# One core, attention with global tokens and a softplus layer: other operands for the fillers, an earlier hold for the loads of batch 1, and a new order of 1,721 jobs

## The chip, the cores and the metric

The kernel runs on one core of a Trainium2 chip. The metric is the device time in microseconds (us) of one execution, the median of several runs. The engines named below are PE (matrix multiply), PEld (its weight loads), DVE (vector), ACT (scalar, with table functions), POOL (general purpose) and SP (which issues most of the loads). A letter q behind an engine's name means its queue of instructions, where DMAs are issued.

## The reference

Eight batches of eight heads of attention, 576 tokens, 64 wide. A token sees its neighbours within 32 positions and eight global tokens; global tokens see everything. Then a two-layer network with softplus over all 4608 tokens.

```python
# q, k, v: (8, 8, 576, 64) float32; global_idx: 8 positions
scores = scale * np.matmul(q, k.transpose(0, 1, 3, 2))
mask = np.abs(pos[:, None] - pos[None, :]) <= 32
mask = mask | is_global[:, None] | is_global[None, :]
scores = np.where(mask, scores, -1000000000.0)
scores = scores - np.max(scores, axis=-1, keepdims=True)
attn = np.exp(scores)
attn = attn / (np.sum(attn, axis=-1, keepdims=True) + 1e-09)
out = np.matmul(attn, v)
# x: (4608, 512), the heads side by side; w_in (512, 2048), w_out (2048, 512)
h = x @ w_in
g = np.maximum(h, 0.0) + np.log1p(np.exp(-np.abs(h)))
return (g @ w_out).astype(np.float32)
```

## The kernel before

**Units of work.** A batch is 18 blocks of 32 tokens. A "pair" is four blocks (128 tokens); there are 36 pairs, and four pairs make one of nine stages m of 512 tokens. For each pair: scores `sc` into PSUM (with the mask added by a matmul `mk` in the first four pairs, by DVE `ma` in the others), row maximum `mx`, subtraction `sub` (not in the first four), exponential `ex`, sum and reciprocal `su`, normalisation `no`, transpose `tp`. The first four pairs do `mx` to `no` in two halves of four heads each. For each batch: loads of q, k and v into `stage` (tiles used by one batch after another), rounding `cast` into `qb`, `kb`, `vb`, transposes into `qx` and `kx`, picking out the global keys and queries (`pick`, `put`, `fill`, `gev`), and the global tokens' own attention: scores `sg`, maximum `mxg`, exponential `gexp`, transpose `tpg` into `pgt`, product `ov`, then `odd`, `both`, `gv`. For the stage: `val` multiplies the probabilities with v into PSUM tiles `xo`, `xev` copies them into xT, the first layer is 16 chunks `h` of four matmuls each, `soft` the softplus into `g`, the second layer `o` four tiles of 16 matmuls, `oev` copies to `osb`, and a DMA stores.

**Batches 0 and 1** are special: q and k come in three pieces each (token ranges t = 0, 1 of 256 tokens, t = 2 of 64), their transposes `tr` are done by PE with an identity, and `trev` (named `turn` in the lists below) copies them out. Stage 0 goes through `val`, `xev` and `h` in three parts of 128, 256 and 128 tokens (`val_0`, `val_1`, `val_2`), stage 1 in two.

**The order.** Each of these steps is a job with a rough cost on each engine that can do it. `_Order` has a list ORDER with one number for each job: five times the job's number plus the engine (0 PE, 1 ACT, 2 DVE, 3 POOL, 4 loads issued by SP). The program walks this list, keeps a clock for each engine from the costs, and emits the jobs in the order of the clock's times. So on each engine the order is that of the list; the modelled times only decide which of the eight PSUM banks a tile takes and where PE fillers stand. Each engine then runs its jobs strictly in order and waits with semaphores for the others.

**Fillers.** Where the model has PE idle for 0.7 us or more, before 34 us of modelled time, `keep` puts in matmuls `warm` that nobody reads: 55% of the gap divided by 220 ns each. Their operands are the first 512 columns of `pgt`, cleared at the start; `pgt` is also where batch 0's `tpg` writes.

**Loads and holds.** SP issues q, k and v; POOL issues the four pieces of `w_in` and the four of `w_out` (each a weight piece converted to 16 bits on the way). Where a load is meant to stay behind a weight piece, `follow` issues a tiny DMA that reads the last values of that piece, so that SP stands still until it has landed. For batch 1 `follow(0, w_in_t[1])` is called with piece x == 0 of the list FIRST, which is q's t = 0; and `follow(1, w_out_t[1])` with half h == 0 of v. The v halves are also made to depend on job `w_out` 1 in the list. The tiny `landed` copy on POOL waits for k's t = 1 of batch 1, and the `w_out` pieces stand behind it.

The order of SP's loads before: batch 0: k t0, k t1, k t2, q t0, q t2, q t1, v half 0, v half 1; batch 1: k t0, k t2, q t0, k t1, q t1, q t2, v half 1, v half 0; then k and q of batch 2, and so on.

Of the kernel before, what the change touches and what calls it, by code (L numbers as in the profile page):

```python
# [19 lines left out]
class _Order:  # L20
# [82 lines left out]
    SHARE = 0.12  # L103
# [27 lines left out]
    WARM = 0  # L131
# [155 lines left out]
def kernel(  # L287
# [242 lines left out]
    if WARM:  # L530
        clear(nc.vector, pgt[:].rearrange("p m i h -> p (m i h)")[:, 0:512])
# [145 lines left out]
    def act(n, psum=True):  # L677
        t = (137 if psum else 270) + .9 * n
        return t - 98, t
# [25 lines left out]
    def fill_in(key, n, thin):  # L705
        ps = psum(key, [P, 512], FP32)
        w = P if thin else 4 * P
        for x in range(n):
            nc.tensor.matmul(out=ps[:, 0:w], lhsT=idle[:, 0:P], rhs=idle[:, 0:w], start=True, stop=True)  # L709
# [39 lines left out]
    def add_parts(b):  # L749
        last = None  # L750
        for x, (w, t) in enumerate(FIRST[b]):
            def emit(e, x=x, w=w, t=t):
                if x == 0 and b:
                    follow(0, w_in_t[1])
# [675 lines left out]
```

## Time and profile before

| | us |
|---|---|
| median of 3 runs (lowest, highest) | 337.99 (337.87, 338.98) |
| the profiled execution | 338.2 |
| its span in the trace | 336.5 |
| PE busy | 316.2 |
| DVE, ACT, POOL busy | 250.0, 224.2, 179.1 |
| mean granted PE clock | 0.975 |

The span runs from the first to the last instruction of the trace; the rest of the execution's time lies around it. Rows of instructions in order of time give the start, the length, the engine, the source line, the operation, output and inputs, and in brackets how long the engine was idle ahead of it and who released it. Lines that stand for several steps: L700 is every copy between tiles, told apart by the tile's name; L1246 is `h`, L1257 `o`, L1211 `val`, L709 the fillers, L1044 the scores, L969 `ov`, L824 the key and query transposes, L958 `tpg`, L1099 `no`, L1108 `tp`, L1080 `ex` of the first four pairs (eight short instructions, of which four carry one half's values and four read the sums), L953 `gexp`, L1067 `sub`, L732 the tiny DMA of `follow`, L494 and L498 the pieces of batches 0 and 1, L444 and L449 the other q, k and v loads, L1308 and L1312 the weights.

### The profile page before, as it was taken

What the parts mean: (1) busy time and instruction counts of PE and PEld (TensorE: products, weight loads), DVE (VectorE), ACT (ScalarE), POOL (GpSimd) and SP (SyncE); (2) the same over time, 40 slices, a digit from 0 to 9 for tenths busy, and PEclk for the clock granted to TensorE, in tenths of its full rate; (3) what the DMA queues carried; (4) which work ended last, traced back from release to release, by engine and by line L of the source; (5) the groups of instructions that cost most, each with busy time, mean ns of one, the idle gap of its engine ahead of it and who ended that gap; (6) DMA issues with size and microseconds to landing.
All of it is one profiled execution on the core that took longest, in us unless ns stands there. A gap on an engine that the chain in (4) does not pass through costs nothing.

```text
span 336.5 us, 12158 instructions
## 1 busy us (share of the span) xinstructions
PE 316.2 (94%) x5286; PEld 170.0 (51%) x5333; DVE 250.0 (74%) x416; ACT 224.2 (67%) x456; POOL 179.1 (53%) x159
## 2 busy tenths in 40 slices
PE   7669899889999999999999999999999999999996
PEld 3426786466555444554554445444544454454453
DVE  6688589968899899998986688788779878460000
ACT  3787767786786859287836786698467665945541
POOL 5554708986386479729865747496631823200000
PEclk9756999999999999999999999999999999999999
DMA  7999998999955989992988997401310030010002
GB/s 182 229 217 238 202 172 138 155 182 193 168 91 103 171 185 174 163 190 59 185 140 167 231 177 176 104 33 49 91 65 2 33 128 33 0 64 33 31 16 109
DMA packets 168733, 42.74 MB, mean 127 GB/s; under 512 B 153192, under 2 KB 165736, under 8 KB 168680
## 3 DMA queue, kind: packets, MB, share of 16 engines
q1 hardware_dynamic: 160664, 28.33, 47.5%
q0 software_dynamic: 6144, 10.49, 13.0%
q10 hardware_dynamic: 1872, 3.15, 2.5%
q8 instruction: 41, 0.67, 0.8%
q14 instruction: 12, 0.10, 0.1%
HBM read 36.71 MB, written 9.44 MB: 137 GB/s over the span
## 4 chain that ended last, share of the span: by engine, by line
PE 61%; DVE 9%; SPq 8%; DMA 8%; POOL 6%; issue 5%; ACT 1%; DVEq 0%; POOLq 0%
PE h L1246 26%; PE o L1257 24%; SPq L444 6%; PE xo L1211 3%; PE s L1044 3%; DMA wout<-in_moe_w_out_dram 3%; POOL pn L1099 2%; DMA stage<-in_q_dram 2%; DMA stage<-in_k_dram 2%; DVE st L1048 2%; DVE m L1061 1%; PE ov L969 1%; DMA stage<-in_v_dram 1%; POOL qb L697 1%; PE warm L709 1%
## 5 line engine op out<-in xcount | busy, mean ns | idle before, releaser
L1246 PE MATMUL h<-xT,win 128*128 128x512 bf16 (+3 forms) x758 | 132.5, 325 | 1.9 <-issue 0.5
L1257 PE MATMUL o<-wout,g 128*128 128x512 bf16 (+1 forms) x560 | 128.3, 373 | 4.7 <-issue 3.3
L1252 ACT ACTIVATE g<-h 128x512 bf16<-128x512 f32 (+3 forms) x192 | 84.3, 500 | 42.2 <-PE h L1246 40.7
L1246 PEld LDWEIGHTS <-win 128*128 128x128 bf16 x768 | 66.5, 98 | 59.4 <-issue 1.4
L1257 PEld LDWEIGHTS <-g 128*128 128x128 bf16 x592 | 55.5, 98 | 62.3 <-issue 1.6
L1067 POOL TENSOR_TENSOR st<-st,m 128x1024 f32<-128x1024 f32 x27 | 52.1, 1933 | 58.0 <-DVE m L1061 49.0
L1099 POOL TENSOR_TENSOR pn<-st,rs 128x1024 bf16<-128x1024 f32 (+1 forms) x32 | 56.7, 1776 | 33.0 <-DVE rs L1093 27.3
L1048 DVE TENSOR_TENSOR st<-s,mask 128x512 f32<-128x512 f32 x64 | 41.1, 676 | 6.9 <-PE s L1044 6.7
L1091 DVE TENSOR_REDUCE sm<-st 128x8 f32<-128x1024 f32 x32 | 38.4, 1199 | 7.3 <-ACT st L1084 7.2
L1061 DVE TENSOR_REDUCE m<-st 128x8 f32<-128x1024 f32 x32 | 38.1, 1201 | 0.3
L1084 ACT ACTIVATE st<-st 128x1024 f32<-128x1024 f32 x32 | 32.7, 1057 | 2.9 <-POOL st L1067 2.3
L700 ACT COPY osb<-o 128x512 f32<-128x512 f32 (+1 forms) x27 | 15.3, 571 | 20.1 <-PE o L1257 15.1
L1108 DVE STREAM_TRANSPOSE pt<-pn 128x512 int32<-128x512 int32 x36 | 24.4, 690 | 3.6 <-POOL pn L1099 3.4
L700 DVE CAST xT<-xo 128x512 bf16<-128x512 f32 (+3 forms) x23 | 12.1, 564 | 13.6 <-PE xo L1211 13.4
L700 ACT CAST xT<-xo 128x512 bf16<-128x512 f32 (+3 forms) x25 | 10.6, 474 | 16.3 <-PE xo L1211 16.1
L697 POOL TENSOR_SCALAR qb<-stage 128x1152 bf16<-128x1152 f32 (+1 forms) x11 | 14.5, 1315 | 9.3 <-DMA stage<-in_q_dram 6.6
L700 POOL CAST kb<-stage 128x1152 bf16<-128x1152 f32 (+1 forms) x12 | 17.2, 1455 | 3.0 <-DMA stage<-in_k_dram 3.0
L1044 PE MATMUL s<-kx,qx 64*32 64x128 bf16 x1152 | 15.8, 229 | 2.1 <-DVE qx L700 0.8
L1044 PEld LDWEIGHTS <-qx 64*32 64x32 bf16 x1152 | 10.9, 94 | 13.3 <-issue 8.9
L1269 POOL DMA_DIRECT2D out_dram<-osb x24 | 14.5, 603 | 5.0 <-ACT osb L700 5.0
L953 ACT ACTIVATE pg<-sg,gnb 128x320 bf16<-128x320 f32 (+1 forms) x32 | 14.9, 581 | 1.5 <-DVE gnb L947 1.5
L1252 ACT ACT_TABLE_LOAD x12 | 15.4, 1283 | 0.7 <-PE h L1246 0.5
(125 smaller groups left out, 312.0 us busy)
## 6 DMA issues: line engine op xcount, KB each, us to landing
stage<-in_v_dram SPq DMA_DIRECT2D x64, 144.0 KB, 4.5
stage<-in_k_dram SPq DMA_DIRECT2D x48, 144.0 KB, 4.3
stage<-in_q_dram SPq DMA_DIRECT2D x48, 144.0 KB, 3.8
out_dram<-osb POOLq DMA_DIRECT2D x24, 256.0 KB, 3.3
out_dram<-osb ACTq DMA_DIRECT2D x11, 256.0 KB, 2.3
stage<-in_k_dram SPq DMA_DIRECT2D x4, 512.0 KB, 6.1
stage<-in_q_dram SPq DMA_DIRECT2D x4, 512.0 KB, 5.6
win<-in_moe_w_in_dram POOLq DMA_DIRECT2D x4, 512.0 KB, 11.2
```

What stands on the lines that cost most here:

```text
L700: {"ACT": nc.scalar.copy, "DVE": V.tensor_copy, "POOL": nc.gpsimd.tensor_copy}[e](out, in_)
L1044: nc.tensor.matmul(out=PS["s", n, g][quad(a ^ g), x, :], lhsT=qx[b % 2][rows(g), a, j * BL:(j + 1) * BL], rhs=kx[b % 2][rows(g), a, e0 * B ...
L1048: V.tensor_tensor(out=PS["st", n][:, h, :, :], in0=PS["s", n, h][:, :, :], in1=mask[:, h, j0:j0 + PB, :, :].rearrange("p j s i -> p j (s i ...
L1061: V.reduce_max(out=m[:], in_=flat(PS["st", n], h0, h1), axis=AX)
L1067: on(e).tensor_tensor(out=t, in0=t, in1=over(PS["m", n, y][:], SL * BL), op=OP.subtract)
L1084: nc.scalar.activation(out=t, in_=t, func=AF.Exp)
L1091: V.reduce_sum(out=sm[:], in_=flat(PS["st", n], h0, h1), axis=AX)
L1099: on(e).tensor_tensor(out=PS["pn", n][:, :, :, h0:h1].rearrange("p x s h -> p h x s"), in0=PS["st", n][:, h0:h1], in1=PS["rs", n, y][:].re ...
L1108: V.transpose(out=bass.AP(base.tensor, base.offset, ap=[list(base.ap[0]), [2 * STEP, PB // 2], [STEP + BL // 2, 2], [1, SL * BL]]), in_=PS ...
L1246: nc.tensor.matmul(out=h[:, :], lhsT=w_in_t[c // 4][:, kd, c % 4 * P:(c % 4 + 1) * P], rhs=PS["xT", m][:, kd, lo:hi], start=(kd == 0), sto ...
L1252: nc.scalar.activation(out=PS["g", m, c][:, lo:hi], in_=PS[key][:, lo_of(c, hi - lo)], func=AF.Softplus)
L1257: nc.tensor.matmul(out=PS["o", m, ns, a][:, :], lhsT=PS["g", m, kf][:, ns * P:(ns + 1) * P], rhs=w_out_t[kf // 4][:, kf % 4, a:z], start=( ...
```

## The change

The fillers read `vb[1]` (four blocks of 128 columns, cleared by DVE at the start) and no longer `pgt`. `follow` now acts once for each of its two tiles, at whichever load comes first in the list: for batch 1 that is the first piece of q or k, behind `w_in` 1, and the first half of v, behind `w_out` 0 instead of 1. Modelled costs of many jobs are other numbers, and so is the share that SP's loads get when both queues run (SHARE). ORDER is a new list throughout; the jobs are the same 1,721, of which 103 are on another engine (as an example, `no` from DVE to POOL five times and back four times, `sub` from POOL to DVE six times and back three times, `xev` 13 times from DVE to ACT and 11 times back). In counts: PE 891 jobs as before, ACT 351 (346), DVE 309 (311), POOL 130 (133), loads 40 as before.

```diff
-    SHARE = 0.12
+    SHARE = 0.55
...
     if WARM:
-        clear(nc.vector, pgt[:].rearrange("p m i h -> p (m i h)")[:, 0:512])
+        nc.vector.memset(vb[1][:, 0:4, 0:2 * D], 0.0)
...
-    idle = pgt[:].rearrange("p m i h -> p (m i h)")
+    idle = vb[1][:, 0:4, 0:2 * D]
...
-            nc.tensor.matmul(out=ps[:, 0:w], lhsT=idle[:, 0:P], rhs=idle[:, 0:w], start=True, stop=True)
+            nc.tensor.matmul(out=ps[:, 0:w], lhsT=idle[:, 0, :], rhs=idle[:, 0, :] if thin else idle, start=True, stop=True)
...
+    followed = set()
+
     def follow(x, t):
+        if x in followed:
+            return
+        followed.add(x)
         nc.sync.dma_start(out=trail[x:x + 1, :], in_=t[0:1, t.shape[1] - 1, t.shape[2] - 2:])

     def add_load(b, w, deps):
-        behind = had(("w_out", 1)) if b == 1 else []
+        behind = had(("w_out", 0)) if b == 1 else []
...
-                    if behind and h == 0:
-                        follow(1, w_out_t[1])
+                    if behind:
+                        follow(1, w_out_t[0])
...
-                if x == 0 and b:
+                if b:
                     follow(0, w_in_t[1])
...
-                T["half", b, h] = o.add({"DMA": (2200 if b else 0, 0)}, emit, deps, rank=0, moves=4000 if b else 2700 + 600 * h, late=LATE if b else 0)
+                T["half", b, h] = o.add({"DMA": (2200 if b else 0, 0)}, emit, deps, rank=0, moves=3300 if b else 2500 + 1100 * h, late=LATE if b else 0)
...
-            T["ex", n, y] = o.add({"ACT": act(k, False) if not masked else (1050, 1150) if n in SUMMED else (1390, 1490)}, lambda e, y=y: ex(e, y), [job, *gate],
+            T["ex", n, y] = o.add({"ACT": act(k, False) if not masked else (1050, 1150) if n in SUMMED else (1390, 1420)}, lambda e, y=y: ex(e, y), [job, *gate],
...
-    for job in o.run(dict(PE=1200 if WARM else 3000, ACT=2600, DVE=2100, POOL=3400, DMA=2700)):
+    for job in o.run(dict(PE=1200 if WARM else 3000, ACT=2600, DVE=2100, POOL=3400, DMA=2300)):
```

What the two lists say for the start, decoded (names as above; the digits behind `ex`, `mx`, `su`, `no` are pair and half, `tr b w t` is batch, 0 for q or 1 for k, token range; "h[128:384]" is a chunk of the second part):

| engine | before | after |
|---|---|---|
| PE | k transposes of batch 0; q t0; mk 0, sc 0; q t2, q t1; mk 1, sc 1; sg 0; sc 3, sc 2; ov 0; val_0; 16 chunks h; val_1; tr 1 k t0; six chunks h[128:384]; val_2; tr 1 q t0; tr 1 k t1, t2; ... sc 5, sc 4 | k transposes of batch 0; mk 0, mk 1; q t0, q t2; sc 0, sc 1; q t1; sg 0; sc 2, sc 3; ov 0; val_0; 11 chunks h; tr 1 k t0; 1 chunk; val_1; tr 1 k t1; 4 chunks; six chunks h[128:384]; val_2; tr 1 q t0; tr 1 k t2; q t2; three chunks; sc 4, sc 5 |
| ACT | ex 0 and ex 1 (both halves); gexp 0; ex 3 (both); ex 2,0; gv 0; two xev 0; ex 2,1; soft | ex 0 and ex 1 (both halves); gexp 0; ex 2,1; odd 0; ex 2,0; ex 3 (both); two xev 0; soft |
| DVE | mxg 0; ...; su 1,1; mx 3,1; tpg 0; mx 3,0; su 0,1; mx 2,1; mx 2,0; odd 0; both 0; tp 0; su 1,0; no 1,0; ... no 3 (both); tp 3; tp 2; casts of batch 1 | mxg 0; mx 2,1; su 1 (both); mx 2,0; tpg 0; su 0,1; mx 3 (both); both 0; gv 0; tp 0; ... tp 1; su 3,0; no 3 (both); tp 2; two casts of k t0; tp 3; a cast of k t1; one xev 1; the cast of k t2; one xev 1 |
| POOL | w_in 0, 1, 2; one cast of v; no 0,0; w_in 3; no 0,1; no 1,1; no 2 (both); clears of batch 1's tiles; three casts of batch 1; landed; w_out 0, 1; a cast; w_out 2; sub 5; sub 4; w_out 3 | w_in 0, 1; two casts of v; w_in 2; no 0 (both); no 1,0; w_in 3; no 1,1; no 2 (both); clears of batch 1's tiles; landed; a cast of k t1; w_out 0, 1, 2; four casts of q; w_out 3; sub 5; sub 4 |
| SP, batch 1 | k t0, k t2, q t0, k t1, q t1, q t2, v 1, v 0 | k t0, k t1, k t2, q t0, q t2, q t1, v 1, v 0 |

In both lists the end is the same: the last tiles of `o`, their copies on ACT and the stores.

More of the change, by code (lines that the diff above doesn't have):

```diff
@@ L746, in add_load @@
             T["load", b, w] = o.add({"DMA": (4400, 0)}, lambda e: load_qk(nc.sync, b, w, (0, 2, 1, 3)), deps, rank=0,
-                                    moves=9200 if w else 8800, late=LATE, behind=had(("load", b - 1, 2)) if b == EARLY else [])
+                                    moves=8500 if b == EARLY else 9000, late=LATE, behind=had(("load", b - 1, 2)) if b == EARLY else [])
     def add_parts(b):
@@ L896, in add_prep @@
                     T["cast", b, w].append(job)
-                    T["turn", b, w][t].append(o.add({"DVE": dve(n), "ACT": act(n)}, lambda eng, w=w, t=t, e=e: trev(eng, w, t, e),
+                    T["turn", b, w][t].append(o.add({"DVE": (620, 710) if t < FULL else (200, 280), "ACT": (630, 740) if t < FULL else (280, 380)}, lambda eng, w=w, t=t, e=e: trev(eng, w, t, e),
                                                     [T["last", w]], rank=at, uses=[k_]))
@@ L911, in add_prep @@
         T["fill", b] = o.add({"DVE": (430, 510), "ACT": (430, 520)}, fill, [T["put", b, 1]] + blanked, rank=rank - 1 if b else 0, uses=[kkey], lead=0 if b else LEAD)
-        T["gev", b] = o.add({"DVE": (150, 240), "ACT": (230, 340)}, gev, [T["put", b]] + blanked, rank=rank - 1 if b else 0, uses=[qkey], lead=0 if b else LEAD)
+        T["gev", b] = o.add({"DVE": (110, 195), "ACT": (150, 200)}, gev, [T["put", b]] + blanked, rank=rank - 1 if b else 0, uses=[qkey], lead=0 if b else LEAD)
     def turned(b, j0, j1):
@@ L990, in add_global @@
         lead = 0 if b else LEAD
-        T["sg", b] = o.add({"PE": (380, 550)}, sg, [x for y in T["turn", b, 1] for x in (y if b < EARLY else [y])] + had(("fill", b), ("gev", b)) + gate, rank=3, array=64, ins=32,
+        T["sg", b] = o.add({"PE": (380, 440) if b else (570, 700)}, sg, [x for y in T["turn", b, 1] for x in (y if b < EARLY else [y])] + had(("fill", b), ("gev", b)) + gate, rank=3, array=64, ins=32,
                            opens=[("sg", key) for key in keys], lead=lead)
@@ L1114, in add_pair @@
         if apart:
-            T["mk", n] = o.add({"PE": (660, 830)}, mk, T["mask"], rank=2, ins=4, opens=[("s", ("s", n, h)) for h in range(2)])
-            T["sc", n] = o.add({"PE": (450, 620)}, sc, ready + had(("mk", n)), rank=0, array=64, ins=64,
+            T["mk", n] = o.add({"PE": (910, 1010)}, mk, T["mask"], rank=2, ins=4, opens=[("s", ("s", n, h)) for h in range(2)])
+            T["sc", n] = o.add({"PE": (550, 630)}, sc, ready + had(("mk", n)), rank=0, array=64, ins=64,
                                uses=[("s", n, h) for h in range(2)], opens=[("st", ("st", n))])
         else:
-            T["sc", n] = o.add({"PE": (280 + 540 * masked, 450 + 540 * masked)}, sc, ready + (T["mask"] + had("make_ends")[:n // TP] if masked else []), rank=3, array=64, ins=64 + 4 * masked,
+            T["sc", n] = o.add({"PE": (280 + 700 * masked, 450 + 700 * masked)}, sc, ready + (T["mask"] + had("make_ends")[:n // TP] if masked else []), rank=3, array=64, ins=64 + 4 * masked,
                                opens=[("s", ("s", n, h)) for h in range(2)] + [("st", ("st", n))])
@@ L1321 @@
     setup("make_band", lambda e: make_band(), {"DVE": (1000, 1080)}, rank=0)
-    setup("make_ident", lambda e: make_ident(), {"DVE": (200, 280)}, [T["make_band"]], rank=0)
+    setup("make_ident", lambda e: make_ident(), {"DVE": (250, 400)}, [T["make_band"]], rank=0)
     setup("make_hot", lambda e: make_hot(), {"DVE": (500, 580)}, [T["make_ident"]], rank=0)
@@ L1329 @@
     setup("make_neg", lambda e: make_neg(), pool(1250), [], rank=0)
-    setup("make_edges", lambda e: make_edges(), {"DVE": (330, 400)}, [T["make_ident"]], rank=1)
+    setup("make_edges", lambda e: make_edges(), {"DVE": (110, 190)}, [T["make_ident"]], rank=1)
     T["slots"] = []
@@ L1391 @@
                 T["w_out", a] = o.add({"POOL": (800, 0)}, lambda e, a=a: weights_out(a),
-                                      [T["landed"], T.get(("w_out", a - 1))], rank=-1, hold=800 if a else 0, moves=3200)
+                                      [T["landed"], T.get(("w_out", a - 1))], rank=-1, hold=800 if a else 0, moves=3100)
         for x in range(len(VALS)):
```

20 lines of the change are left out of this document (10 added, 10 removed), and 144 rows, old and new, of the table ORDER.

## The prediction

> **What bounds the kernel now.** First the shares of the page, then the busy time by stretch (columns: stretch, its length, busy time and instruction count of PE, PEld, DVE, ACT, POOL, the granted PE clock, the DMA share, GB/s).
>
> ```profile
> PE 316.2 (94%) x5286; PEld 170.0 (51%) x5333; DVE 250.0 (74%) x416; ACT 224.2 (67%) x456; POOL 179.1 (53%) x159
> ...
> 10.00:20.00 10.00, 6.31 (x148) 4.01 (x150) 7.53 (x18) 7.81 (x33) 6.63 (x11) 0.67 1.30 227
> 20.00:30.00 10.00, 7.47 (x150) 2.93 (x152) 8.54 (x22) 7.78 (x38) 3.84 (x5) 0.50 1.24 203
> 30.00:40.00 10.00, 8.90 (x236) 7.93 (x239) 7.13 (x17) 7.69 (x31) 8.00 (x15) 0.98 1.13 238
> ...
> 110.00:130.00 20.00, 19.52 (x360) 9.71 (x367) 19.04 (x29) 14.71 (x24) 12.52 (x11) 1.00 0.91 182
> 130.00:150.00 20.00, 19.33 (x461) 10.34 (x466) 19.65 (x30) 12.31 (x22) 11.98 (x9) 1.00 0.95 173
> ```
>
> PE is the bound from about 31 us on; before that it runs in half-clock scraps while ACT, DVE and the loads prepare the first tokens. DVE is nearly as full between 110 and 150 us, which matters below. Next, what PE waits for from 60 us to the end (us in total, times, longest):
>
> ```profile
> PE o L1257 <- issue: 3.2, 20, 0.2
> PE o L1257 <- DMA wout<-in_moe_w_out_dram: 0.8, 1, 0.8
> PE h L1246 <- issue: 0.5, 3, 0.2
> ```
>
> Apart from the 3.7 us in gaps of 0.16, which follow other array shapes and stay with any sequence that mixes them, only one wait is worth having: 0.8 us for the last piece of w_out. So whatever is gained must be gained before 64 us, and kept afterwards. The PE rows of that stretch in order of time (start, length, what; in brackets the idle time ahead and what ended it):
>
> ```profile
> 25.14 1.31 PE L969 MATMUL ov<-vb,pgt 32*32 32x129 bf16 x72 [0.96 <-DVE pgt L960]
> 26.78 3.19 PE L709 MATMUL warm<-pgt 128*128 128x512 bf16 x7 [0.33 <-issue]
> 29.90 0.44 PE L1211 MATMUL xo<-pt,vg 32*64 32x128 bf16 x8
> 31.02 3.87 PE L1246 MATMUL h<-xT,win 128*128 128x128 bf16 x64
> 34.94 0.59 PE L709 MATMUL warm<-pgt 128*128 128x512 bf16 x2
> 36.22 0.32 PE L1211 MATMUL xo<-pt,vg 32*64 32x256 bf16 x8 [0.68 <-DVE pt L1108]
> 36.33 0.86 PE L1211 MATMUL xo<-pt,vb 32*64 32x32 bf16 x80
> 37.12 0.40 PE L824 MATMUL tr<-ident,kb 128*128 128x128 bf16 x4
> 38.13 2.79 PE L1246 MATMUL h<-xT,win 128*128 128x256 bf16 x24 [0.21 <-DVE xT L700]
> 63.15 0.81 PE L1257 MATMUL o<-wout,g 128*128 128x512 bf16 x3 [0.84 <-DMA wout<-in_moe_w_out_dram]
> ```
>
> Useful work starts at 31.02; between 34.89 and 36.22 PE has only fillers or nothing (1.33 us), because the transposes of pairs 1 and 2 are late.
>
> **The change part by part.** *Costs in the order's model* (SHARE, moves, the pairs of numbers): no instruction changes by them; they set how many fillers stand where and which PSUM bank is taken. Price 0.
>
> *Fillers on vb[1] instead of pgt.* The false dependence goes: batch 0's transpose into pgt waited for a filler (DVE and ACT in order of time).
>
> ```profile
> 24.22 0.51 DVE L958 STREAM_TRANSPOSE pgt<-pg 128x320 int32<-128x320 int32 x1 [1.20 <-PE warm L709]
> 15.47 0.37 ACT L1080 ACTIVATE st<-s,m 128x128 f32<-128x128 f32 x1
> 18.59 0.37 ACT L1080 ACTIVATE st<-s,m 128x128 f32<-128x128 f32 x1 [0.22 <-DVE m L1059]
> 21.34 1.90 ACT L953 ACTIVATE pg<-sg,gnb 128x320 bf16<-128x320 f32 x4
> 30.68 0.43 ACT L700 CAST xT<-xo 128x128 bf16<-128x128 f32 x2 [1.11 <-PE xo L1211]
> 31.00 0.38 ACT L1080 ACTIVATE st<-s,m 128x128 f32<-128x128 f32 x1
> 32.54 1.28 ACT L1252 ACT_TABLE_LOAD   x1
> ```
>
> The 1.20 us is not all won. What is late next is ACT. Two of its eight exponentials of the first four pairs run from 18.59 to 21.34, 1.38 each. In the old list the last one stands behind xT (31.00); in the new list all eight stand ahead of it. New chain: the mask matmuls come before the query's transposes, so I put the first exponential 0.3 earlier, at 15.2; four end at 20.7; the global one (1.90) waits for its maximum, about 20.9, and ends near 22.8; one exponential to 24.2. DVE, with two row maxima ahead of it, transposes into pgt from about 22.6; ov followed 0.92 behind that start (25.14 less 24.22), so 23.5, and ends 1.31 later at 24.8; fillers in front of it may cost 0.2: 25.0. Then the copy of odd, now on ACT, 0.55 (an estimate, from xT's 0.43, also two copies) to 25.6; three exponentials to 29.7; xT 0.43. First h at 30.3 against 31.02: -0.7. The new clear of vb[1] has twice the elements in half the width of the old one; I take it as unchanged, at most a filler more or less while keys are still loading. POOL's clear of the ones in vb[1] may now wait for fillers; it stands at about 30.4, by when the first h has ended the fillers, so 0 to 0.4, and POOL's next piece waits for a load anyway.
>
> *The sequence, 31 to 40 us.* With the exponentials done near 29.7 instead of 32.5 (where ACT loads the next table), pairs 1 to 3 finish earlier.
>
> ```profile
> 31.51 1.04 POOL L1099 TENSOR_TENSOR pn<-st,rs 128x512 bf16<-128x512 f32 x1 [2.87 <-DVE rs L1093]
> 32.65 2.17 DVE L1099 TENSOR_TENSOR pn<-st,rs 128x512 bf16<-128x512 f32 x2
> 34.86 1.31 DVE L1108 STREAM_TRANSPOSE pt<-pn 128x512 int32<-128x512 int32 x2
> ```
>
> (POOL and DVE in order of time.) POOL normalises pair 2 in two pieces of 1.04 from about 28.3 to 30.4; DVE does both halves of pair 3 (2.17) from about 30 and then transposes pair 2 (half of 1.31): 32.8. PE gets there later: 12 of the 16 chunks of h (0.24 each, 2.9 us) and the first key transposes of batch 1 (37.12 to 38.13 less the wait, 0.8) end at 34.0. So val_1 finds its data, and the 1.33 us go; then the other two key transposes (0.8) and four chunks (0.95) cover the evacuation behind val_1, and the 0.21 at 38.13 goes as well. -1.5, if the loads are there.
>
> *Loads of batch 1: whichever piece goes first now waits for w_in[1], and both halves of v wait for w_out[0].* (SP in order of time, then the tile view of win, then the page's list of DMA issues with the median landing last.)
>
> ```profile
> 15.21 0.65 SPq L494 DMA_DIRECT2D stage<-in_k_dram  x1
> 27.74 0.73 SPq L732 DMA_DIRECT2D trail<-win  x1
> 51.60 12.07 SPq L444 DMA_DIRECT2D stage<-in_k_dram  x8
> L1308 POOL DMA_DIRECT2D win<-in_moe_w_in_dram x4: 765/790/992, 15.8 to 21.0; - x4
> DMA to landing us min/median/max: 8.5/11.2/12.3
> stage<-in_k_dram SPq DMA_DIRECT2D x4, 512.0 KB, 6.1
> wout<-in_moe_w_out_dram POOLq DMA_DIRECT2D x4, 512.0 KB, 8.6
> ```
>
> In the old order a k piece of 512 KB and one of 64 KB were issued at 15.21, ahead of the small DMA at 27.74 that waits for w_in[1]. Now SP stops first. Without 0.576 MB beside it, at the 203 GB/s of the stretch, w_in[1] lands at most 2.8 us earlier: SP goes on between 24.9 and 27.74. The second k piece is issued about 1.5 later (the small DMA 0.73, one issue 0.65) and lands, at the median 6.1, between 32.5 and 35.3. PE asks for it at about 34.9 (val_1 from 34.0, 0.9), and after landing come a POOL copy and cast, some 0.8 by the length of its neighbours: wait 0 to 1.2. The 64 KB piece, one place on, holds DVE's cast ahead of an xT copy: another 0 to 0.5. I take 0.4 for both, nearer the early landing, since both full queues shared the engines in the old order. The fourth w_in piece goes from 21.0 to about 26.5 on POOL, behind one more normalisation; landing at its least, 8.5, is 35.0, at its most 38.8; PE wants it at about 35.7, so 0 to 3.1, and I take 0, since SP no longer fills the engines ahead of it. Two halves of v behind w_out[0] are eight issues instead of four after the wait: w_out[0] is issued near 34 to 35 and lands 8.6 later, 43, SP needs some 7 us (before: 3.2 for four), so the loads of batch 2 start at 50 instead of 51.6. Nothing waits for that gain on PE; price 0.
>
> The Trainium skill, DMA: Bandwidth & Descriptors, section on queues, rings and completion order, says each DMA engine takes its queues in turn, packet by packet, and elsewhere on that page that issuing from several engines adds no bandwidth. By that, holding the k piece back only swaps who is late, which speaks against this edit; it would leave my sum at the upper end of the waits above (1.7 instead of 0.4; 336.7). The 1.30 DMA share at 227 GB/s in the row of 10 to 20 us agrees that the engines were full.
>
> *w_out[3].*
>
> ```profile
> 51.74 3.75 POOL L1067 TENSOR_TENSOR st<-st,m 128x1024 f32<-128x1024 f32 x2 [11.49 <-DVE m L1061]
> 55.44 0.79 POOL L1312 DMA_DIRECT2D wout<-in_moe_w_out_dram  x1
> ```
>
> On POOL it stood behind two subtractions, which waited 11.49 for DVE; in the new list it stands ahead of them, behind casts of batch 1 that are done near 41. Landing by 52: the 0.84 at 63.15 goes. -0.8.
>
> **The sum.** -0.7 - 1.5 - 0.8 + 0.4 = -2.6. The profiled execution took 338.2 (span 336.5 and 1.7 around it), 0.2 above the median of the runs, 338.0. So 335.6 for that execution, **335.4** as a median.
>
> **Rivals.** *A, no change: DVE takes it back.* PE arriving 2 us early is worth nothing if DVE, busy 19.04 and 19.65 of 20 us from 110 to 150, cannot bring the pairs early. Then PE waits for xo or s there and the end stays at 338.0. For it: those two rows. Against: pair 4 and 5's scores come earlier in the new PE list, so DVE starts its own full stretch earlier too. Chance 0.2.
>
> *B, slower: the held k piece.* If w_in[1] does not land earlier, the second k piece is issued at 29.2; at the longest landing of a weight piece here, 12.3, it is there at 41.5, and PE, in order, stands at its transposes from 34.9 to 42.3. That is 7.4; less the 3.0 of gains, 342.4. It decides from a landing at 38.1 on, where the wait (4.0) is 1.0 more than the gains. Against it: 6.1 median for such a piece. Chance 0.17, mostly near 339.5.
>
> *C, more: the clock comes earlier.* Rows: granted 0.50 from 20 to 30 us, 0.98 after, with seven fillers in a row from 26.78. In the new list fillers no longer hold up pgt and a gap of some 3.5 us ahead of ov may be filled; then ov runs at twice the rate and ACT's chain is 0.65 shorter; with no load wait (0.4) as well, 334.3. Chance 0.1. The Trainium skill (TensorE: Matmul & The Clock Gate, "The HAM clock gate") says the full clock comes after one busy window of about 3.4 us; the fillers from 26.78 to the full-rate h at 31.02 agree, and by that rule this rival needs nearly the whole gap filled.
>
> **How the numbers follow.** The forecast has 0.53, C 0.10, A 0.20, B 0.17. 1.0 us (0.3%) is about what this kernel's runs can tell. Faster 0.63, same 0.2, slower 0.17. Low end: C with 0.7 to spare for gaps of 0.16 that a better mix saves, 333.6. High end: B at its common size, 339.5. The forecast's own range, with the load waits between 0 and 1.7 and the first h between 30.1 and 30.6, is 334.6 to 337.0.
>
> **What would show it.** Right: no DVE wait for a filler before pgt; first h near 30.3; no fillers between the chunks of h and val_1; no PE wait for w_out near 62; SP's first k piece of batch 1 issued after the small DMA, at 25 to 28. Wrong: PE waiting for tr or h behind k pieces or w_in at 35 to 40; new waits of PE for DVE between 100 and 150; a first h after 32, since the clock or ACT's eight exponentials were misjudged.

## The result and the profile after

The changed kernel took 341.37 us (median of 4 runs, 340.85 to 343.27), the kernel before 338.05 beside it (337.87 to 338.98): a ratio of 1.0103, 95% interval 1.006 to 1.0146. It is slower by 1%, where 335.4 us had been forecast. The profiled span is 339.5 us against 336.5: 3.0 more to be explained. All ratios here and below leave out executions in a slower state of the chip, so a ratio need not be the quotient of the medians given.

First what PE waits for from 60 us to the end, in the changed kernel.

```profile
PE pick L858 <- DVE qb L695: 1.0, 1, 1.0
PE s L1049 <- DVE kx L700: 0.7, 2, 0.5
PE pick L871 <- DVE picked L700: 0.5, 1, 0.5
```

The 0.8 us for w_out is gone; 2.2 us of small waits for DVE stand in its place. Then PE's rows in order of time (start, length, what; in brackets the idle time ahead and what ended it).

```profile
22.47 0.91 PE L974 MATMUL ov<-vb,pgt 32*32 32x129 bf16 x72
...
28.52 2.67 PE L1251 MATMUL h<-xT,win 128*128 128x128 bf16 x44 [1.62 <-ACT xT L700]
33.41 0.40 PE L829 MATMUL tr<-ident,kb 128*128 128x128 bf16 x4 [2.22 <-DVE kb L700]
...
34.30 0.81 PE L709 MATMUL warm<-vb 128*128 128x512 bf16 x3
35.05 0.43 PE L1216 MATMUL xo<-pt,vg 32*64 32x256 bf16 x6
35.73 0.30 PE L1216 MATMUL xo<-pt,vg 32*64 32x256 bf16 x2 [0.26 <-ACT kx L700]
...
44.53 0.29 PE L1049 MATMUL s<-kx,qx 64*32 64x128 bf16 x11
47.45 0.66 PE L1049 MATMUL s<-kx,qx 64*32 64x128 bf16 x53 [2.63 <-issue]
...
52.63 0.22 PE L1251 MATMUL h<-xT,win 128*128 128x128 bf16 x1
55.02 0.34 PE L1251 MATMUL h<-xT,win 128*128 128x128 bf16 x3 [2.17 <-issue]
```

The first layer starts at 28.52, which is 2.50 earlier than before (31.02). Then PE stands three times: 2.22 us for a piece of k, 2.63 in the middle of pair 4's scores and 2.17 in the middle of a chunk of h. The last two are marked "issue": nothing that the profile shows was waited for, and the stop cuts a run of matmuls whose operands were there (11 of 64 scores done, then 53). Between the first h and 60 us PE is idle for 1.76 of 28.98 us before and for 7.45 of 31.48 after:

```profile
31.02:60.00 28.98, 27.22 (x624) 1.00 1.04 185
```

```profile
28.52:60.00 31.48, 24.03 (x589) 1.00 1.14 207
```

So 2.5 us earlier, then 5.7 more of idling: about 3.2 behind at 60 us, and 3.0 at the end.

**The stream of instructions.** What can stop PE in the middle of a run? The page's list of DMA queues has a line that the prediction had not looked at:

```profile
q8 instruction: 41, 0.67, 0.8%
```

That is 41 transfers of 16 KB. Counting PE's instructions in the trace against the landings of these blocks, PE stops after 1470 and after 1726 rows, that is matmuls and weight loads (they differ by 256), and goes on 1.5 us after a block has landed (1.3 to 1.5 in the stops of the table). The landings below are the ends of the DMA records of that queue; A is the block that PE needs after row 1470 (1472 in the expectation of e7), B the one after row 1726 (landing; us since the block ahead of it; where PE stopped and went on, for stops over 0.25 us).

```
                       A landed  gap   PE stopped       B landed  gap   PE stopped
before                 46.1      7.3   47.10 to 47.42   49.9      3.8   -
after                  46.0      6.5   44.82 to 47.45   53.5      7.6   52.85 to 55.02
e1_before_fill_vb      45.6      7.6   45.50 to 46.95   49.4      3.9   -
e2_after_fill_pgt      45.7      6.2   44.75 to 47.11   52.5      6.8   52.51 to 53.85
e3_.._behind_wout1     46.5      7.0   44.81 to 47.99   52.2      5.6   -
e4_.._pieces_free      44.8      6.7   43.94 to 46.27   51.8      7.0   -
e5_.._no_v1_loads      46.7      6.2   46.25 to 48.26   52.3      5.6   -
e6_.._one_wout_load    43.3      3.5   -                47.5      4.3   -
e7_.._short_fillers    43.6      6.6   43.79 to 44.87   49.7      6.1   -
e8_.._fill_wout3       44.5      7.9   45.41 to 46.03   50.9      6.3   50.90 to 52.23
e9_.._wout_spread      43.6      4.7   -                50.7      7.1   50.38 to 51.97
e10_.._pieces_free     45.3      4.1   46.26 to 46.70   51.7      6.4   52.10 to 53.17
e11_.._wout_spread     43.5      6.2   -                50.9      7.4   49.93 to 52.36
e12_.._vb_again        44.3      7.6   45.18 to 45.75   48.7      4.5   -
```

The kernel before already stood 0.32 us at A: its row `[0.32 <-issue]` at 47.42, in scores too. It came to row 1470 at 47.10, hardly before the block could be used. Both kernels pass row 1214, where the block ahead of A begins, at the same time (40.95 before, 40.98 after), and A lands 5.1 and 5.0 us later. But the changed kernel has only 3.8 us of work in these 256 rows, where the kernel before had 6.2: it came to row 1470 2.3 us earlier, and the block did not. In eleven of these kernels A lands 4.4 to 6.2 us after PE has passed row 1214; in the three that take w_out's later pieces out of the changed kernel's stretch (e6, e9, e10) it lands 2.0 to 2.9 us after it.

The Trainium skill (Runtime: NRT & Kernel Launch, "Instruction fetch mechanics") says that an engine's instructions are refilled in blocks of 16 KiB, 256 instructions, while the current one runs, and that crossing a boundary is "mostly hidden". The trace agrees on the size (41 packets, 0.67 MB; stops 256 rows apart) and not on the cost: 2.63 and 2.17 us.

### The profile page after: what moved, and what is told of

It reads as the page before. It is cut to its first block, busy times and chain, and to the rows that moved or that the text cites. A ratio compares the mean times of both kernels' runs of the same rounds, so it can differ in the third digit from the quotient of the medians.

```text
span 339.5 us, 12213 instructions
## 1 busy us (share of the span) xinstructions
PE 319.3 (94%) x5336; PEld 169.4 (50%) x5336; DVE 250.8 (74%) x416; ACT 222.9 (66%) x457; POOL 170.9 (50%) x156
## 4 chain that ended last, share of the span: by engine, by line
PE 78%; SPq 9%; DMA 7%; issue 3%; DVE 1%; ACT 1%; ACTq 0%; POOLq 0%
PE o L1262 35%; PE h L1251 32%; SPq L444 5%; PE xo L1216 4%; DMA stage<-in_v_dram 3%; PE s L1049 3%; DMA win<-in_moe_w_in_dram 2%; DMA stage<-in_k_dram 2%; PE ov L974 2%; SPq L449 1%; SPq L498 1%; DVE qb L695 1%; PE pick L858 1%; PE tr L829 1%; SPq L494 1%
## 5 line engine op out<-in xcount | busy, mean ns | idle before, releaser
L1251 PE MATMUL h<-xT,win 128*128 128x512 bf16 (+3 forms) x768 | 135.8, 326 | 4.0 <-issue 2.3
L1262 PE MATMUL o<-wout,g 128*128 128x512 bf16 (+1 forms) x592 | 136.6, 374 | 0.0
L1257 ACT ACTIVATE g<-h 128x512 bf16<-128x512 f32 (+3 forms) x192 | 85.6, 501 | 44.7 <-PE h L1251 42.7
L1072 POOL TENSOR_TENSOR st<-st,m 128x1024 f32<-128x1024 f32 x24 | 46.6, 1952 | 52.5 <-DVE m L1066 50.1
L700 ACT COPY osb<-o 128x512 f32<-128x512 f32 (+1 forms) x29 | 16.7, 576 | 16.8 <-PE o L1262 15.1
L700 ACT CAST xT<-xo 128x512 bf16<-128x512 f32 (+3 forms) x27 | 11.5, 477 | 18.7 <-PE xo L1216 18.6
L700 POOL CAST vb<-stage 128x1152 bf16<-128x1152 f32 x14 | 16.9, 1215 | 9.1 <-PE xo L1216 5.4
L1049 PE MATMUL s<-kx,qx 64*32 64x128 bf16 x1152 | 15.2, 224 | 4.4 <-issue 2.6
L700 DVE CAST xT<-xo 128x512 bf16<-128x512 f32 (+3 forms) x21 | 11.3, 567 | 10.2 <-PE xo L1216 10.1
L697 POOL TENSOR_SCALAR qb<-stage 128x1152 bf16<-128x1152 f32 (+2 forms) x12 | 12.8, 1074 | 4.7 <-DMA stage<-in_q_dram 2.4
L951 DVE TENSOR_REDUCE gm<-sg 128x1 f32<-128x320 f32 (+1 forms) x32 | 12.3, 446 | 3.2 <-PE sg L941 3.2
```

The source lines that it names most:

```text
L700: {"ACT": nc.scalar.copy, "DVE": V.tensor_copy, "POOL": nc.gpsimd.tensor_copy}[e](out, in_)
L1049: nc.tensor.matmul(out=PS["s", n, g][quad(a ^ g), x, :], lhsT=qx[b % 2][rows(g), a, j * BL:(j + 1) * BL], rhs=kx[b % 2][rows(g), a, e0 * B ...
L1072: on(e).tensor_tensor(out=t, in0=t, in1=over(PS["m", n, y][:], SL * BL), op=OP.subtract)
L1251: nc.tensor.matmul(out=h[:, :], lhsT=w_in_t[c // 4][:, kd, c % 4 * P:(c % 4 + 1) * P], rhs=PS["xT", m][:, kd, lo:hi], start=(kd == 0), sto ...
L1257: nc.scalar.activation(out=PS["g", m, c][:, lo:hi], in_=PS[key][:, lo_of(c, hi - lo)], func=AF.Softplus)
L1262: nc.tensor.matmul(out=PS["o", m, ns, a][:, :], lhsT=PS["g", m, kf][:, ns * P:(ns + 1) * P], rhs=w_out_t[kf // 4][:, kf % 4, a:z], start=( ...
```

## The experiments

Theory: the loads of 34 to 55 us fill the DMA engines, PE's next block of instructions lands late behind them, and all that the new order gains is lost there; beside it the held k piece costs some 2 us. Rivals: the fillers; the hold alone; the place of the v loads; the late-coming DVE.

**e1: the fillers alone, in the kernel before.**

```diff
-        clear(nc.vector, pgt[:].rearrange("p m i h -> p (m i h)")[:, 0:512])
+        nc.vector.memset(vb[1][:, 0:4, 0:2 * D], 0.0)
...
-    idle = pgt[:].rearrange("p m i h -> p (m i h)")
+    idle = vb[1][:, 0:4, 0:2 * D]
```

> The old list with only the fillers' operand changed to vb[1]. If the false dependence between fillers and pgt cost time, the transpose into pgt no longer waits 1.20 for a filler, first h comes about 1.0 earlier (near 30.0 instead of 31.0) and the time is about 337.0. If something else is late next (ACT's exponentials, the transposes of pairs 1 and 2), first h stays within 0.3 and the time stays at 338.0.

337.5 us, ratio to before 0.9941 (0.9905 to 0.9977). PE in order of time:

```profile
24.27 1.18 PE L969 MATMUL ov<-vb,pgt 32*32 32x129 bf16 x72
...
29.43 1.74 PE L1246 MATMUL h<-xT,win 128*128 128x128 bf16 x26
...
46.95 0.40 PE L1044 MATMUL s<-kx,qx 64*32 64x128 bf16 x27 [1.45 <-issue]
```

The first h comes 1.6 earlier, but 1.1 of it goes at block A (stall 1.45 instead of 0.32), and behind the stall the granted clock is 0.50 from 48.3 to 51.7, so that the profiled span, 336.7, is no shorter than before. By the ratio this edit alone is no loss.

**e2: the fillers on `pgt` again, in the changed kernel** (e1's lines the other way).

> The new list with the fillers reading pgt again. If the earlier first h of the changed kernel (28.5 against 31.0) is the fillers' doing, it goes back by 1 us or more, to 29.5 to 30.5, but the end moves by less, since PE then waits at 33 us for keys anyway: 341.4 to 342.4. If it is the sequence's doing, nothing moves: 341.4.

340.99 us, 1.0066 (1.0028 to 1.0104). The first h stands at 28.78 with the old fillers too: in the new list the early start is the sequence's doing. Both stalls stay (2.36 and 1.35).

**e3: the loads of v behind w_out's second piece, as before.**

```diff
-        behind = had(("w_out", 0)) if b == 1 else []
+        behind = had(("w_out", 1)) if b == 1 else []
...
-                        follow(1, w_out_t[0])
+                        follow(1, w_out_t[1])
```

> The new list with batch 1's v halves behind w_out[1] again instead of w_out[0]. Theory of the instruction stream (PE's blocks of instructions come late when the loads fill the DMA engines): SP starts v some 3 us later, the block that PE lacked at 52.9 comes sooner, the stall of 2.17 there shrinks below 0.7 and the time is 339.4 to 340.4. Rival (the stall is set by how fast PE uses up instructions, whatever else is loaded): both stalls stay within 0.5 and the time is 341.4 or more, because the loads of batch 2 come later.

341.08 us, 1.0082 (1.0033 to 1.0131). Block B lands earlier (52.2 instead of 53.5) and its stall is gone, yet the time stays above the 339.4 to 340.4 of the theory. A is later, and behind its stall the granted clock is 0.50 from 47.3 to 54.1 (the 53 scores take 0.94 instead of 0.66), so that PE comes to B only at 55.9, long after the landing. The stall at B went in part because PE was late:

```profile
33.01 0.40 PE L829 MATMUL tr<-ident,kb 128*128 128x128 bf16 x4 [1.52 <-DVE kb L700]
...
47.99 0.94 PE L1049 MATMUL s<-kx,qx 64*32 64x128 bf16 x53 [3.18 <-issue]
```

**e4: the k pieces not held** (the hold only at the list's first entry, as before).

```diff
-                if b:
+                if x == 0 and b:
                     follow(0, w_in_t[1])
```

> The new list with the old hold for q and k of batch 1: only q's first piece calls the tiny DMA, so all three k pieces go ahead of w_in[1]. Theory of the held piece: PE's wait of 2.22 for the keys at 33 us and the 1 us behind it go; w_in[1] then lands later than 25.4, at 28 to 30, and first h moves by 0 to 1.5; the time is 339.0 to 340.5. Rival (the first 36 us are bound by the bytes to be loaded, whichever goes first): what the keys gain the weights lose, first h at 30 or later, the time stays at 341.4 or rises.

341.03 us, 1.0054 (1.0013 to 1.0095).

```profile
28.77 4.30 PE L1251 MATMUL h<-xT,win 128*128 128x128 bf16 x44 [1.58 <-ACT xT L700]
...
46.27 0.94 PE L1049 MATMUL s<-kx,qx 64*32 64x128 bf16 x53 [2.33 <-issue]
```

The wait for the k piece is gone, as the theory wants; but the 44 matmuls took 4.30 instead of 2.67, at half clock. PE comes 0.9 earlier to the block, the block lands 1.2 earlier (44.8), and PE still stands 2.33; behind that the clock is half again from 46.3 to 49.7 (0.94 for the scores). The median falls between the two forecasts and the interval overlaps the changed kernel's, so the hold is at most a part of the loss.

**e5: the v loads of batch 1 left out** (batch 1 then uses batch 0's v), to see whether they delay the blocks.

```diff
-                    load_v(nc.sync, b, h, range(R))
+                    if b != 1:
+                        load_v(nc.sync, b, h, range(R))
```

> The new list, with the eight loads of batch 1's v left out (the cast takes batch 0's v again). In the changed kernel PE stalled at 44.8 to 47.5 and at 52.9 to 55.0 for its own instructions, whose blocks of 256 rows landed at 46.3 and 53.8. Theory of the instruction stream under load: the second block, asked for while the v loads fill the DMA engines, lands by 51 instead of 53.8 and the second stall goes; the first stays at 2 to 3 us. Rival (a fixed time for each block, 6.5 to 7 us): both stay, 53 to 54.

A single execution: 339.89 us, span 338.2. The stall at B is gone, the one at A stays (2.02), and the wait for the k piece is longer (3.36). So A is not the v loads' doing. For B the run says less: SP issues batch 2's k in their place, at 45.58 instead of 54.61, the DMA share from 46 to 52 us stays at 1.23 to 1.31, and the block lands at 52.3, not by 51 as expected.

**e6: one piece of w_out loaded and used four times**, so that three transfers of 512 KB are left out and the second layer's values are others.

```diff
-    w_out_t = [wts.tile(... name=f"wout{i}") for i in range(KF // 4)]
+    w_out_t = [wts.tile(... name=f"wout{i}") for i in range(1)] * (KF // 4)
...
     def weights_out(a):
+        if a:
+            return
```

> The new list, with only the first of the four w_out pieces loaded and used four times. Theory of the instruction stream under load: the block that landed at 46.3 was asked for at about 39.8, when three more w_out pieces and q's pieces were under way; with 3 MB less to read it lands by 44 and the stall before 47.5 shrinks from 2.6 to below 0.8. Rival (a fixed time for each block): the block lands at 46 or later and the stall stays at 2 us or more.

A single execution: 336.1 us, span 334.4, 5.1 less than the changed kernel's. PE's instructions are the same ones; A lands 3.5 us after its forerunner instead of 6.5, and PE passes without a stop:

```profile
33.01 0.40 PE L829 MATMUL tr<-ident,kb 128*128 128x128 bf16 x4 [1.98 <-DVE kb L700]
...
44.79 0.75 PE L1049 MATMUL s<-kx,qx 64*32 64x128 bf16 x64
```

The stretch from 42 to 46 us (length, busy time and count of PE, PEld, DVE, ACT, POOL, clock, DMA share, GB/s), first the changed kernel, then this one:

```profile
42.00:46.00 4.00, 2.82 (x71) 2.29 (x68) 1.31 (x3) 3.15 (x10) 0.00 (x0) 1.00 1.19 194
```

```profile
42.00:46.00 4.00, 4.00 (x145) 3.48 (x132) 2.00 (x5) 3.24 (x10) 0.00 (x0) 1.00 0.40 93
```

PE idles where the DMA engines are full, and does not where they are at 0.40.

**e7: each filler as two of half the width**, about the same time of fillers with 64 more rows of PE.

```diff
-        for x in range(n):
-            nc.tensor.matmul(out=ps[:, 0:w], lhsT=idle[:, 0, :], rhs=idle[:, 0, :] if thin else idle, start=True, stop=True)
+        for x in range(2 * n):
+            nc.tensor.matmul(out=ps[:, 0:2 * P], lhsT=idle[:, 0, :], rhs=idle[:, 0:2], start=True, stop=True)
```

> The new list, with each filler as two of half the width: the same PE time, some 64 rows more in PE's instructions. If a block's end at a fixed row count (1472 rows, between the 10th and 12th scores matmul of pair 4 in the changed kernel) is what PE waits at, the stall now comes some 32 matmuls earlier in the program, in the transposes or chunks ahead of pair 4's scores, and PE still goes on only at 47 to 48. If the stall belongs to the place in the program (the scores, a PSUM bank, a tile), it stays inside pair 4's scores.

A single execution: 352.14 us, span 350.4.

```profile
24.90 0.30 PE L974 MATMUL ov<-vb,pgt 32*32 32x129 bf16 x7 [1.46 <-issue]
...
44.87 0.21 PE L832 MATMUL tr<-ident,qb 64*64 64x64 bf16 x1 [1.08 <-issue]
...
47.69 1.05 PE L1049 MATMUL s<-kx,qx 64*32 64x128 bf16 x64
...
149.40 0.25 PE L1049 MATMUL s<-kx,qx 64*32 64x128 bf16 x8 [2.49 <-issue]
184.70 0.24 PE L1049 MATMUL s<-kx,qx 64*32 64x128 bf16 x5 [2.78 <-issue]
220.89 0.23 PE L1049 MATMUL s<-kx,qx 64*32 64x128 bf16 x1 [1.96 <-issue]
```

The stops move to other work: pair 4's scores run through, the transposes just ahead of them stop instead, `ov` (row 702) and a chunk of h (row 1214, 1.13) stop as well, and new stops come at 149, 185, 221 and 257 us, each 1.2 to 1.5 after a block landed (148.1, 183.3, 219.6, 255.8). A stall thus belongs to a count of instructions, not to what they read. PE goes on at 44.87, not at 47 to 48 as expected: it passed row 1214 at 38.7, and A landed 4.9 us after that.

The late stops show a second thing. Those at 221 (1.96) and 257 (1.72) come while the DMA engines are nearly idle:

```profile
240.00:280.00 40.00, 37.70 (x606) 18.76 (x611) 31.34 (x52) 27.43 (x44) 14.38 (x10) 1.00 0.05 19
```

There a block lands 2.1 us after PE has passed the row 256 ahead and PE goes on some 1.4 later, but PE runs through the 256 rows, nearly all of them short, in 1.2 and 1.5 us. So full DMA engines lengthen a stop and are not its only cause; what counts is which 256 rows fall between two block ends. The four late stops are 8.95 of the 10.9 us that the span is longer.

**e8: e1 with w_out's last piece issued ahead of `sub` 5 and 4**, the prediction's last gain by itself.

> The old list with the fillers on vb[1] and one entry moved: the issue of w_out[3] ahead of the two subtractions of pairs 5 and 4. The wait of 0.84 for w_out near 62 us goes; w_out[3] is then read between 41 and 52 us, beside the v and k loads and PE's instruction blocks. Theory of the instruction stream under load: a block in that stretch comes up to 2 us later, and of the 0.8 little is left: 0.993 to 0.998 of the time before. Rival (the wait was the price): 0.8 less than the old list with fillers on vb[1], 0.990 to 0.993 of the time before.

340.42 us, 0.9983 (0.9936 to 1.0029). No wait for w_out, but a stop at B that e1 did not have:

```profile
52.23 0.70 PE L1044 MATMUL s<-kx,qx 64*32 64x128 bf16 x59 [1.33 <-issue]
```

The price at 52 is seen (DMA share 1.26 to 1.27 from 48 to 52 us, 0.68 to 0.79 in e1), the gain is not: e1 itself, coming later, had no wait for w_out. This execution also stops for instructions at 273 us, 2.29 in `val`, with half clock for 3.4 us behind it; e1 does not, and why is open. The time is at the upper edge of the theory's range.

**e9 to e11: w_out spread out.** In e9 the changed kernel's second and third pieces go behind the q casts of batch 1 and a tiny copy that waits for the first, the fourth behind `sub` 5 and 4 as in the kernel before; PE's list is untouched. e10 adds e4's edit. e11 does the like to e1: its later pieces and its second half of v stand behind the first piece.

```diff
     def weights_out(a):
+        if a == 1:
+            nc.gpsimd.tensor_copy(seen[:, 1, :], w_out_t[0][:, 3, d_model - 1:d_model])
```

> The changed kernel with its loads spread out: w_out's second and third pieces are issued behind the four casts of batch 1's q and behind a tiny POOL copy that waits for the first piece to land, and the fourth is issued as late as in the kernel before. Nothing is left out. Theory (PE's next block of instructions waits behind the loads on the DMA engines): with less on the DMA engines between 38 and 47 us the block that ends at 46.3 lands earlier, some 43 to 45, and PE's stall in pair 4's scores shrinks from 2.6 us to under 1; the later block may be later instead, since the loads come then. Sum: about 2 us less than the changed kernel, ratio to before about 1.000 to 1.005. Rival (the stall belongs to what PE's instructions wait for, not to the loads): the stall stays at 2 us or more and the time at 1.005 to 1.010. A second rival: the projection of the output waits for the late pieces, some 1 to 3 us between 55 and 75, and the time is no better.

> The run before with one edit more: the pieces of batch 1's k are not held for w_in. Nothing is left out. Theory (two separate losses, the held k piece and the block of instructions): the wait of PE's transposes for k's cast goes (2.2 us in the changed kernel), and the stall of PE in pair 4's scores is under 1; first h between 28.5 and 28.9. Some 3 to 4 us less than the changed kernel, ratio to before 0.992 to 1.000. Rival (PE only comes earlier to the same block): the block lands at 45 to 46 all the same, the stall is 2 us or more, and the time 1.000 to 1.008, as the changed kernel with the pieces free alone gave 1.0054.

> The kernel before with its fillers on the idle tile of batch 1's v (as in the first run), and w_out's second piece issued later, behind the last q cast of batch 1, the rest of w_out and the loads of v behind the landing of w_out's first piece. Nothing is left out. Theory: the stall of 1.45 us that the first run kept in pair 4's scores at 47 us shrinks to under 0.5, since its block lands 1 to 2 us earlier; ratio to before 0.988 to 0.994. Rival: the block that comes after it is the late one, or the late w_out pieces are waited for at 60 to 65 us (the kernel before waited 0.84 for the last one): ratio 0.994 to 1.000, no better than the first run.

e9: 338.71 us, 1.0009 (0.9969 to 1.005), span 336.7. PE in order of time, and the same stretch as above:

```profile
33.48 0.40 PE L829 MATMUL tr<-ident,kb 128*128 128x128 bf16 x4 [2.46 <-DVE kb L700]
...
44.89 0.75 PE L1049 MATMUL s<-kx,qx 64*32 64x128 bf16 x64
...
51.97 0.34 PE L1251 MATMUL h<-xT,win 128*128 128x128 bf16 x3 [1.59 <-issue]
```

```profile
42.00:46.00 4.00, 4.00 (x152) 3.49 (x143) 1.91 (x4) 3.23 (x10) 1.67 (x3) 1.00 0.31 36
```

With every load still done, only later, A lands at 43.6, the 2.63 are gone, and so is nearly the whole loss against the kernel before. B still stops PE for 1.59, since the loads stand in its way now, and nothing waits for a piece of w_out.

e10: 338.67 us, 0.9994 (0.9956 to 1.0032). That is the edge of both ranges: the k wait is gone, yet a piece of w_in is late instead and the granted clock is 0.50 from 29.0 to 35.8 us; both stops remain, smaller.

```profile
32.05 2.74 PE L1251 MATMUL h<-xT,win 128*128 128x128 bf16 x24 [0.99 <-DMA win<-in_moe_w_in_dram]
...
46.70 0.66 PE L1049 MATMUL s<-kx,qx 64*32 64x128 bf16 x53 [0.44 <-issue]
...
53.17 0.34 PE L1251 MATMUL h<-xT,win 128*128 128x128 bf16 x3 [1.07 <-issue]
```

e11: 340.22 us, 1.0045 (1.0007 to 1.0084): the rival named the place, but the time is beyond its 1.000 too. A comes in time (43.5), B is the late one:

```profile
52.36 0.70 PE L1044 MATMUL s<-kx,qx 64*32 64x128 bf16 x59 [2.43 <-issue]
```

Behind 60 us one more stop for instructions follows (us in total, times, longest), at 273 us, as in e8, and half clock from 276.7 to 280.1:

```profile
PE xo L1211 <- issue: 2.5, 1, 2.5
```

**e12: e1 once more.**

> The first run's kernel once more (the kernel before with its fillers, their idle tile and its clearing on batch 1's v alone), beside the run before it on the same chip. Theory: as then, first h near 29.4, PE's stall in pair 4's scores near 1.4 us, ratio 0.990 to 0.998. Rival (the first run's gain was the chip's scatter): 0.998 to 1.002.

337.62 us, 0.9972 (0.9933 to 1.0011), span 333.9, stall at A 0.57. With e1's 0.9941 it is the best of the whole kernels tried: some 0.3 to 0.6% faster than before, and the second interval alone reaches 1. The two profiled executions of this one kernel differ by 2.8 us of span: a stall at A of 1.45 against 0.57, half clock behind it (48.3 to 51.7) in e1 alone, and a stop of 0.47 at 79 us in e1 alone. So one execution's stop is sure to no better than 0.9 us; that A lands 0.5 later in e3 may mean nothing, while the 2.63 that are missing in e6 and e9 are well beyond it.

## Why the prediction was wrong

*The range and rival B.* The time lies above the range's end of 339.5. It falls between rival B's 339.5 and 342.4, but by chance: B needed the second k piece at 38.1 or later, and its cast began at 34.98. B had the right sign and, in part, the right place (a held k piece), but not the larger sum. (The forecast's own low end, 334.6, should be 334.8 by its terms; nothing hangs on it.)

*First h, -0.7: right in kind, too small.* No wait for a filler is left ahead of pgt, and ACT is the chain that ends last, as the step said. But ACT was 1.6 us faster than worked out; in order of time:

```profile
14.57 0.37 ACT L1085 ACTIVATE st<-s,m 128x128 f32<-128x128 f32 x1 [0.55 <-DVE m L1064]
...
20.06 1.96 ACT L958 ACTIVATE pg<-sg,gnb 128x320 bf16<-128x320 f32 x4
...
28.14 0.50 ACT L700 CAST xT<-xo 128x128 bf16<-128x128 f32 x2
```

The first exponential starts at 14.57 instead of 15.2, the first four run without a break into the global one at 20.06 instead of 20.9, and xT follows at 28.14 instead of 29.7. With that `ov` starts at 22.47, not 23.5, and since the granted clock is full from 22.8 on it takes 0.91, not 1.31. The early clock is rival C's part, though no gap of 3.5 us was filled for it: PE had real work and four fillers without a break from 17.52 on. Measured: -2.50. In e1, with the old list, the fillers alone gave -1.6.

*The sequence, -1.5, and the load wait, +0.4: the second was mis-sized.* SP was freed where the step put it; the rows of SP, then DVE and POOL:

```profile
25.44 0.73 SPq L737 DMA_DIRECT2D trail<-win  x1
26.27 2.28 SPq L494 DMA_DIRECT2D stage<-in_k_dram  x2
...
43.63 0.64 SPq L737 DMA_DIRECT2D trail<-wout  x1
44.37 10.13 SPq L449 DMA_DIRECT2D stage<-in_v_dram  x8
54.61 8.36 SPq L444 DMA_DIRECT2D stage<-in_k_dram  x7
```

```profile
32.92 0.76 DVE L700 CAST kb<-stage 128x512 bf16<-128x512 f32 x2 [2.29 <-DMA stage<-in_k_dram]
...
34.98 0.43 DVE L700 CAST kb<-stage 128x512 bf16<-128x512 f32 x1 [0.68 <-DMA stage<-in_k_dram]
```

```profile
35.01 0.44 POOL L1394 COPY seen<-stage 128x1 f32<-128x1 f32 x1 [5.30 <-DMA stage<-in_k_dram]
```

The second k piece landed inside the window given (34.98, of 32.5 to 35.3), and PE did not wait for it. It waited for the first, which the step gave no price at all: PE asked at 31.19, 2.0 before the 33.2 of the forecast, because h itself was 1.8 earlier, and the piece came at 32.9 as SP allowed. Thus what the first step won beyond its 0.7 was lost at once: 2.22. The gap ahead of val_1 did go (0.26 left), though three fillers still stand there, against the forecast. w_in's last piece cost nothing, as assumed. The v loads took SP 10.13 us, not 7, and batch 2's k is at 54.61 instead of 50; the price of 0 held.

What that step drew from the Trainium skill (DMA: Bandwidth & Descriptors, "Queues, rings and completion order"), that holding a piece back only swaps who is late, came true in kind: the w_in pieces took 7.0 us at the median instead of 11.2, k's 8.2 instead of 6.1.

```profile
stage<-in_k_dram SPq DMA_DIRECT2D x4, 512.0 KB, 8.2
win<-in_moe_w_in_dram POOLq DMA_DIRECT2D x4, 512.0 KB, 7.0
wout<-in_moe_w_out_dram POOLq DMA_DIRECT2D x4, 512.0 KB, 10.4
```

*w_out's last piece, -0.8: right where it was looked for, worth nothing.* It is not waited for any more. But e8, with the same move, has a stop of 1.33 at block B, and e9, with the piece back behind `sub`, has no wait for it either.

*The step that failed: "PE is the bound", with no term for its instructions.* The sum held every engine and every data transfer, but not the blocks of PE's own instructions, which ride on the same DMA engines. They cost 4.80 in the changed kernel against 0.32 before: +4.5. "Kept afterwards" was asked of DVE (rival A) only. The 0.32 stood in the trace of before at 47.42, marked "issue", cutting a run of 32 scores; it was passed over. With it the forecast would have had a floor: as long as the loads stand where they do, the 256 rows from 1214 to 1470 take about 6.5 us (5.0 until the block has landed, 1.5 until PE goes on), however little work is in them.

The terms as measured: -2.5 first h; +2.2 k piece; +4.5 stream of instructions; the kernel before's other idle time of 31 to 60 us (1.4, of which 0.9 ahead of val_1 and h) against 0.4, -1.0; w_out -0.8; small waits for DVE and ACT behind 60 us 2.2 against 1.1, +1.1. Together +3.5, where the span shows +3.0; the rest was not followed up.

*The gaps of 0.16 us.* The prediction took 3.7 us of them for the mark of mixed array shapes. They are records that the trace lacks. The groups of the second layer, before and after:

```profile
L1257 PE MATMUL o<-wout,g 128*128 128x512 bf16 (+1 forms) x560 | 128.3, 373 | 4.7 <-issue 3.3 <-DMA wout<-in_moe_w_out_dram 0.8 <-ACT st L1084 0.2
```

```profile
L1262 PE MATMUL o<-wout,g 128*128 128x512 bf16 (+1 forms) x592 | 136.6, 374 | 0.0
```

Both kernels issue 592; where all are recorded the gaps are gone. e1 and e12 show it on one kernel: 3.3 us of such gaps ahead of `o` in e1, whose trace lacks 44 matmuls, and none in e12, which has all. This had no part in the sum, only in the low end of the range.

*Rival A* is seen only faintly: the small waits at 110 to 140 us. They do not grow when PE comes earlier: 2.2 us for DVE behind 60 us in the changed kernel, 2.0 in e6, whose span is 5.1 shorter. *What stays open:* when exactly PE asks for a block (the trace shows its packet and its landing), and why e8 and e11 stop at 273 us and e1 and e12 do not. It was not tried whether e9 with the v loads spread out too would pass block B and beat e1.

## What to carry to other kernels

An "issue" gap of more than a microsecond inside a run of equal matmuls is a sign that PE waits for its own instructions: count PE's rows up to it, and see whether the next such gap stands 256 rows on and behind a landing in the "instruction" queue. Where a new order puts 256 short rows together, ask how long the next block needs: here some 6.5 us with the DMA engines full, 3.3 to 3.6 with them nearly idle (e7). If they are full, move loads that nobody needs yet (here the second to fourth piece of w_out) out of the stretch first. And before adding up gains, follow each one to the next thing that PE asks for: 2 us earlier at a transpose is 2 us of waiting, if its load is held.

## What was not expected of the hardware

- Block A lands 2.0 to 2.9 us after PE has passed the row 256 ahead in the three kernels that take w_out's later pieces out of the changed kernel's way (e6, e9, e10), and 4.4 (e5, e11) to 6.2 (e1) in the others, though its one packet takes only 0.9 to 1.1; PE goes on 1.3 to 1.5 us after the landing in each of the stops in the table.
- The granted clock at the first chunks of h was full in the changed kernel, e3, e5, e6 and e9 (44 matmuls in 2.67) and half in e4 (4.30), with the same instructions of PE ahead of them and starts within 0.5 us: 1.6 us by the clock's state alone.
- After stops of 1.1 to 3.2 us the granted clock was 0.50 for 3.4 us in e1, e4, e7 (twice), e8 and e11, and for 6.8 us in e3; in the changed kernel, with stops of 2.63 and 2.17, it stayed full. Half clock for 3.4 us is up to 1.7 us of PE's work, so equal stops can cost unequal times.
